# Windowed attention and expert layer on one core: transposing the attention weights with VectorE and SBUF transfers in place of TensorE

## The chip, the core and the metric

The kernel runs on one core of a Trainium2 chip. The engines are named as in the profile: PE (TensorE: matrix products, and transposes as a product with an identity), DVE (VectorE), ACT (ScalarE), POOL (GpSimd) and SP (SyncE, which here issues every transfer). Each engine works through its own queue in order and waits at an instruction whose inputs are not there yet. SBUF is the on-chip memory of 128 partitions, PSUM the memory into which PE writes. The metric is the device time of one execution in microseconds, median of several runs; smaller is better.

## The reference

Four batches, eight heads of 64, 768 positions. Each query sees the keys closer than 16 positions and 24 block summaries (the maximum over 32 keys, the mean over 32 values). The result feeds a gated layer with a squared ReLU.

```python
k_sum = k.reshape(B, H, nb, 32, D).max(axis=3)
v_sum = v.reshape(B, H, nb, 32, D).mean(axis=3)
scores_l = np.where(abs(pos[:, None] - pos[None, :]) < 16, scale * q @ k.T, -1e9)
scores_s = scale * einsum('bhsd,bhnd->bhsn', q, k_sum) + log(32)
a = softmax(concatenate([scores_l, scores_s], axis=-1))
x = (a @ concatenate([v, v_sum], axis=2))      # heads side by side: [4, 768, 512]
xk = mu_k * x + (1 - mu_k) * x_prev
xr = mu_r * x + (1 - mu_r) * x_prev
out = sigmoid(xr @ w_r) * (relu(xk @ w_k) ** 2 @ w_v)
```

## The kernel before

The work falls into **units** and **halves**. A unit (`unit`, L420) is one pair of heads of one batch over one half of the positions, 384 of them: 32 units in all, eight for each batch. It runs like this. `scores` (L441) multiplies queries with 120 columns for each window of 64 queries: 96 neighbouring keys and the 24 block maxima. DVE adds the mask and finds the maximum (L452), ACT takes the exponential (L456), DVE the reciprocal of the sum (L462, L463), POOL scales the weights (L468). The weights `y` now have the queries on the partitions. The product with the values needs the keys there, so PE transposes them: three 128x120 transposes for each head (L475) into the one PSUM buffer `pt`, from where ACT copies them to `pts` (L479). `values` (L488) multiplies `pts` with the values, and DVE or ACT copies the result out (L499, L501).

A half (n = 0 to 7: batch n // 2, first or second half of its positions) is the expert layer: mixing (L510 to L524), the gate (L542 to L544, then the sigmoid L533), and for each of eight chunks a first product (L580), ReLU and square (L587, L589), a split into a high and a low part (L593, L595) and a second product (L606). From half 1 on, a product is made of three in a fast format, out of high and low parts; half 0 uses plain products, which need more time, since the weights have not been split by then (`single`, L567).

Block summaries of the values come, in batch 0, from PE (L380, L400). In batches 1 to 3 they come from a load of the transposed values (L391) into a buffer `st`, a sum on DVE and a small transpose (L395); SP then broadcasts them into the value tiles (L415: 24 rows, six runs of 128 numbers each). The buffers `st`, three of them, are also those into which the weights are loaded (L306).

**What sets the order.** No order is written by hand. `Plan.op` records every operation with its engine, what it reads and writes, and a due time; `Plan.schedule` (L138) then goes through a modelled time and each time issues the operation that can start first, by due time where several can. The lengths come from the table `LENGTH` (L39), the due times from `gate_due`, `e1_due`, `e2_due` and the dues handed to `unit`: half n is due at `GATE1 + PERIOD * (n - 1)`, and the eight units of the next batch are due `UNITS` apart ahead of their gate. Buffers are given out by this plan too. Its result fixes the order on every engine; on the chip the engines wait for each other with semaphores. In the plan, SP needs 60 ns for an issue (L213). `warm` products (L660) fill gaps of PE in the first 110 us of the plan.

Of the kernel before, what the change touches and what calls it, by code (L numbers as in the profile page):

```python
# [20 lines left out]
P = 128  # L21
# [18 lines left out]
    score=900, transpose=340, vtrans=200, vpool=900, vsel=240, spread=560, spread_p=900, values=1000, gate=2790, gate32=930, e1=2090, e1_32=2800,  # L40
    e2a=1400, e2b=700, e2=700, e2_32=2800, e2l_32=930,
    warm=220, kred=860, kred2=470, kmax=190, kcopy=340, vred=860, mask=204, rc=310, evac=475, mixd=535, sub=475, khv=300,
    result=695, wbits=340, wor=612, wsub=612, tiny=60,
    exp=380, pts=380, vm=160, mixa=520, cast=405, relu=525, square=530, sigmoid=500, sigmoid3=4000, wscale=570, wcast=530,
    norm=345, wscale_p=640, wcast_p=640, mixa_p=860, kcopy_p=630, evac_a=375, fill=735,
# [7 lines left out]
STEP0 = 6800  # L53
GATE1 = 92000
PERIOD = 52000
# [4 lines left out]
GAP = 300  # L60
# [40 lines left out]
class Plan:  # L101
# [36 lines left out]
    def schedule(self):  # L138
# [16 lines left out]
        dma = port = 0  # L155
# [10 lines left out]
        while any(ready.values()):  # L166
            best = None
            for e, now in engines.items():
# [3 lines left out]
                for o, at in ready[e]:  # L172
                    if o.name == "warm":
                        fill = max(now, at), o
                        continue
                    start, need, ok = max(at, now, o.due - EARLY if e == "SP" else 0), {}, True
                    for x in o.bufs:
# [14 lines left out]
                    key = (start if late else now, o.due, o.n)  # L192
# [9 lines left out]
            o.cost, o.emit = o.ways[e]  # L202
            for f in o.ways:
                ready[f] = [x for x in ready[f] if x[0] is not o]
# [4 lines left out]
            if e == "PE" and start < COLD:  # L209
                o.cost *= 1.6  # L210
            o.start = start
            if e == "SP":
                engines[e] = start + 60  # L213
                dma = max(dma, start + 600) + o.size * DMA_NS_PER_BYTE
                o.finish = dma + DMA_FIXED - 600
            else:
# [20 lines left out]
def tile_kernel(ctx: ExitStack, tc: tile.TileContext, q, k, vT, v, mask, ident, pool, sel, mu, w_k, w_v, w_r, out):  # L237
# [7 lines left out]
    def slots(name, n, shape):  # L245
# [8 lines left out]
        vs=tiles("vs", 1, [P, NS]), vm=tiles("vm", 4, [P, P]), sp=tiles("sp", 2, [P, P]),  # L254
        y=tiles("y", 4, [P, NSL, NK]), mn=tiles("mn", 4, [P, NSL]), sm=tiles("sm", 3, [P, 2 * NSL]),
        rc=tiles("rc", 3, [P, 2 * NSL]), pts=tiles("pts", 3, [NK, NSL, P]),
# [163 lines left out]
    def unit(b, p, hf, e, due):  # L420
# [9 lines left out]
        pt = [buf("pt") for _ in range(2)]  # L430
        pts = [buf("pts") for _ in range(2)]
# [14 lines left out]
        op("PE", "score", due - 10000, scores, reads=[*e["kparts"], (kt, "s"), (qt, 0)],  # L446
           writes=[(sc[0], 0), (sc[1], 0)])
        for h in range(2):
            for i in range(NSL):
# [3 lines left out]
                    out=y[h].t[:, i, :], in0=sc[h].t[:, i, 0:NK], in1=mask_sb[:, var, :], scale=-SCALE, scalar=3.0e38,  # L453
# [3 lines left out]
                    y[h].t[:, i, :], y[h].t[:, i, :], AF.Exp, bias=mn[h].t[:, i:i + 1], scale=-1.0,  # L457
# [8 lines left out]
        for h in range(2):  # L466
            for i in range(NSL):
                op("POOL", "norm", None, lambda h=h, i=i: nc.gpsimd.tensor_scalar(  # L468
                    out=y[h].t[:, i, :], in0=y[h].t[:, i, :], scalar1=rc.t[:, NSL * h + i:NSL * h + i + 1],
# [3 lines left out]
            def transposes(h=h):  # L473
                for i in range(NSL):
                    nc.tensor.transpose(out=pt[h].t[0:NK, i * P:(i + 1) * P], in_=y[h].t[:, i, :], identity=ident_sb)  # L475
# [3 lines left out]
            op("ACT", "pts", None, lambda h=h: nc.scalar.copy(  # L479
                out=pts[h].t, in_=pt[h].t[0:NK, 0:NSL * P].rearrange("p (i c) -> p i c", c=P)),  # L480
               reads=[(pt[h], 0)], writes=[(pts[h], 0)])

        def values():
            for w in range(HW):
                i, c = divmod(w, 2)
                for h in range(2):
                    hs = slice(h * D, (h + 1) * D)
                    nc.tensor.matmul(  # L488
                        av.t[hs, w * QW:(w + 1) * QW], windows(vw)[:, w, hs], pts[h].t[:, i, c * QW:(c + 1) * QW],
# [14 lines left out]
    def mix(b, hf, which, p):  # L504
# [14 lines left out]
        if first:  # L519
            return xa  # L520
# [44 lines left out]
    def experts(b, hf, x, z):  # L565
# [4 lines left out]
        def first(j):  # L570
# [20 lines left out]
            if single:  # L591
                return
# [189 lines left out]
```

## Time and profile before

| what | value |
|---|---|
| median of 3 runs | 461.58 us (461.45 to 462.07) |
| the profiled execution, whole | 462.56 us |
| its span, first to last instruction | 460.8 us |
| mean granted PE clock | 0.999 |
| PE transposes of weights, L475 | 192, of 128x120 |
| ACT copies of them, L479 | 64, of 120x384 |
| transfers of queue q1 | 24183 packets, 51.35 MB, 32.5% of 16 engines |
| packets under 512 B | 2935 |

The rows of the page and of the trace are shown with the prediction. A row of a group reads: line, engine, operation, output and inputs by the program's names, shapes and count; then busy time and the mean of one in ns; then the idle time of the engine ahead of it and who ended most of it. A row of the chain or of the timeline begins with the start and the length in us. The profiled execution lasts 1.8 us longer than its span.

### The profile page before, as it was taken

Reading aid. Unit: us, or ns where it says so; the run is one execution under the profiler, and the core shown is the slowest. Engines: PE = TensorE matmul, PEld = TensorE weight load, DVE = VectorE, ACT = ScalarE, POOL = GpSimd, SP = SyncE. Lnnn points to the kernel's source line nnn. Section 1 sums busy time; section 2 is a strip of 40 time slices with the busy share of each in tenths; the row PEclk is TensorE's granted clock in tenths of the full one; section 3 lists DMA queues with packets and bytes.
Section 4 is the critical chain, followed back from the end, with each engine's and each line's share of the span. In section 5 each row is a group of like instructions: output and inputs, shape, how many; then the busy total and the mean of one; then the engine's idle time right before and its main releaser. Section 6 shows DMA issues by size and latency. Waiting matters only on the chain.

```text
span 460.8 us, 9597 instructions
## 1 busy us (share of the span) xinstructions
PE 449.6 (98%) x3510; PEld 363.2 (79%) x3510; DVE 254.7 (55%) x846; ACT 288.1 (63%) x811; POOL 112.3 (24%) x238
## 2 busy tenths in 40 slices
PE   8999999988999999999999999999999999999996
PEld 8755655556788888987788888987788889988895
DVE  4789798963642566365444478357364455131213
ACT  3878989876875657258976558248977565232221
POOL 0762565622334002004343002104242201000000
PEclk9999999999999999999999999999999999999999
DMA  8963598652202067036002049017000010001001
GB/s 279 396 228 119 184 324 284 232 209 67 75 8 61 1 224 302 1 91 229 16 14 63 1 130 392 4 43 271 19 16 14 0 70 0 1 1 68 1 0 70
DMA packets 24230, 51.96 MB, mean 113 GB/s; under 512 B 2935, under 2 KB 10743, under 8 KB 24183
## 3 DMA queue, kind: packets, MB, share of 16 engines
q1 hardware_dynamic: 24183, 51.35, 32.5%
q8 instruction: 28, 0.46, 0.4%
q14 instruction: 19, 0.16, 0.1%
HBM read 43.28 MB, written 6.29 MB: 108 GB/s over the span
## 4 chain that ended last, share of the span: by engine, by line
PE 88%; ACT 7%; POOL 2%; SPq 1%; DVE 1%; issue 1%; DMA 0%; POOLq 0%; ACTq 0%
PE mm L606 29%; PE mm L580 28%; PE pt L475 5%; PE av L488 5%; PE sc L441 4%; PE mm L542 4%; PE mm L543 4%; PE mm L544 4%; ACT y L456 3%; PE mm L555 2%; PE pt L660 2%; POOL y L468 2%; ACT L456 1%; ACT pts L479 1%; PE mm L380 1%
## 5 line engine op out<-in xcount | busy, mean ns | idle before, releaser
L580 PE MATMUL mm<-xs,w 128*128 128x384 f32 x736 | 149.8, 352 | 0.0
L580 PEld LDWEIGHTS mm<-xs,w 128*128 128x128 f32 x736 | 130.4, 188 | 12.5 <-issue 1.4
L468 POOL TENSOR_SCALAR y<-y,rc 128x120 f32<-128x120 f32 x192 | 91.2, 493 | 167.5 <-DVE rc L463 138.7
L606 PE MATMUL mm<-w,kh 128*128 128x512 f32 x336 | 91.8, 402 | 0.0
L587 ACT ACTIVATE r<-mm 128x384 f32<-128x384 f32 x64 | 31.2, 487 | 91.9 <-PE mm L580 91.8
L456 ACT ACTIVATE y<-y,mn 128x120 f32<-128x120 f32 x192 | 73.5, 385 | 12.2 <-DVE mn L452 11.9
L606 PEld LDWEIGHTS mm<-w,kh 128*128 128x128 f32 x336 | 60.7, 188 | 11.2 <-issue 0.2
L593 DVE CAST kh<-r 128x384 fp32r<-128x384 f32 x44 | 16.1, 365 | 75.2 <-ACT r L589 75.1
L452 DVE CUSTOM_DVE_ANT_0 y<-sc,mask_sb 128x120 f32<-128x120 f32 x192 | 42.4, 277 | 25.1 <-PE sc L441 22.7
L606 PE MATMUL mm<-w,kl 128*128 128x512 f32 x168 | 52.3, 406 | 0.0
L524 DVE TENSOR_TENSOR xs<-xa,xs 128x384 fp32r<-128x384 f32 x56 | 30.1, 552 | 29.5 <-ACT xs L522 29.2
L479 ACT COPY pts<-pt 120x384 f32<-120x384 f32 x64 | 30.3, 474 | 14.8 <-PE pt L475 13.3
L516 DVE SCALAR_TENSOR_TENSOR xa<-vx,mu_sb,xa 128x384 f32<-128x384 f32 x56 | 33.7, 628 | 6.2 <-ACT xa L510 5.4
L456 ACT ACTIVATION_READ_ACCUMULATOR y<-y,mn 128x1 f32 x192 | 36.2, 189 | 0.0
L475 PE MATMUL pt<-ident_sb,y 128*120 128x128 f32 x192 | 32.7, 279 | 3.0 <-POOL y L468 2.5
L542 PE MATMUL mm<-w,xs 128*128 128x512 f32 x84 | 33.6, 399 | 2.0 <-ACT z L533 2.0
L606 PEld LDWEIGHTS mm<-w,kl 128*128 128x128 f32 x168 | 30.1, 188 | 6.1
L589 ACT ACTIVATE r<-r 128x384 f32<-128x384 f32 x64 | 33.6, 524 | 1.1
L488 PEld LDWEIGHTS av<-pts,vx 120*64 120x64 f32 x768 | 25.2, 137 | 11.4 <-issue 10.0
L475 PEld LDWEIGHTS pt<-ident_sb,y 128*120 128x120 f32 x192 | 22.3, 137 | 15.1 <-POOL y L468 6.4
L595 DVE TENSOR_TENSOR kl<-r,kh 128x384 fp32r<-128x384 f32 x56 | 31.8, 568 | 4.1 <-ACT kh L594 1.1
L544 PE MATMUL mm<-w,xs 128*128 128x512 f32 x84 | 32.8, 391 | 0.0
(66 smaller groups left out, 539.7 us busy)
## 6 DMA issues: line engine op xcount, KB each, us to landing
vx<-in_v SPq DMA_DIRECT2D x32, 384.0 KB
kt<-in_k SPq DMA_DIRECT2D x15, 544.0 KB
qt<-in_q SPq DMA_DIRECT2D x32, 192.0 KB
out<-z SPq DMA_DIRECT2D x24, 256.0 KB
st<-in_vT SPq DMA_DIRECT2D x12, 384.0 KB
st<-in_w_k SPq DMA_DIRECT2D x8, 512.0 KB
st<-in_w_v SPq DMA_DIRECT2D x8, 512.0 KB
st<-in_w_r SPq DMA_DIRECT2D x4, 512.0 KB
```

Source lines behind the costliest of these rows:

```text
L452: op("DVE", "mask", None, lambda h=h, i=i, var=var: nc.vector.tensor_tensor_reduce(out=y[h].t[:, i, :], in0=sc[h].t[:, i, 0:NK], in1=mask_ ...
L456: op("ACT", "exp", None, lambda h=h, i=i: nc.scalar.activation(y[h].t[:, i, :], y[h].t[:, i, :], AF.Exp, bias=mn[h].t[:, i:i + 1], scale=-1.0,
L468: op("POOL", "norm", None, lambda h=h, i=i: nc.gpsimd.tensor_scalar(out=y[h].t[:, i, :], in0=y[h].t[:, i, :], scalar1=rc.t[:, NSL * h + i: ...
L475: nc.tensor.transpose(out=pt[h].t[0:NK, i * P:(i + 1) * P], in_=y[h].t[:, i, :], identity=ident_sb)
L479: op("ACT", "pts", None, lambda h=h: nc.scalar.copy(out=pts[h].t, in_=pt[h].t[0:NK, 0:NSL * P].rearrange("p (i c) -> p i c", c=P)), reads= ...
L488: nc.tensor.matmul(av.t[hs, w * QW:(w + 1) * QW], windows(vw)[:, w, hs], pts[h].t[:, i, c * QW:(c + 1) * QW], start=True, stop=True,)
L516: op("DVE", "mixd", None, lambda: nc.vector.scalar_tensor_tensor(out=xa.t, in0=xt.t[:, 1 + lo:1 + lo + HT], scalar=mu_sb[:, which, p:p + 1 ...
L542: nc.tensor.matmul(ps.t, xh.t[:, ts], h, start=(p == 0), stop=False)
L544: nc.tensor.matmul(ps.t, xl.t[:, ts], h, start=False, stop=(p == NPAIR - 1))
L580: nc.tensor.matmul(ps.t[:, 0:HT], w.t[:, p * P:(p + 1) * P], (x[p] if single else x[p][s]).t, start=(n == 0), stop=(n == len(terms) * NPAI ...
L589: op("ACT", "square", None, lambda: nc.scalar.activation(r.t, r.t, AF.Square), reads=[(r, 0)], writes=[(r, 0)])
L606: nc.tensor.matmul(acc[t].t, a.t[:, t * P:(t + 1) * P], v.bitcast(F32) if single else v, start=start, stop=stop)
```

## The change

In batches 1 to 3 the weights are no longer transposed by PE. The tile `y` gets 128 columns in place of 120 (eight zeros each, set once by POOL). DVE transposes each head's 128x384 weights within blocks of 32x32 into a buffer `st`, two instructions a unit (`flip`). That leaves each block transposed where it stood; block (r, c) has yet to go to row block r, column block c. Sixteen transfers a unit, all issued by SP, do that (`move`): one for each pair (c, r), 32 partitions (24 for the last r) by six runs of 32 numbers. The values then read `pts`, of which there are two whole ones (one unit each). Batch 0 keeps PE's transposes and ACT's copies. In the first half, six of the eight chunks stay plain, and two use the split form (`PLAIN`), so that its mixed inputs are split too. The table of lengths, the due times and the scheduler's rules change: an issue on SP costs 450 ns in the plan, at most eight transfers are under way, and a change of ACT's function table has a price.

```diff
+    norm=345, wcast_p=640, mixa_p=600, kcopy_p=450, evac_a=375, flip=470,
...
-STEP0 = 6800
-GATE1 = 92000
-PERIOD = 52000
+STEP0 = 4800
+PLAIN = 6, 6
+GATE1 = 80000
+PERIOD = 51000
...
-EARLY = 15000
+EARLY = 20000
+AHEAD = 22000
+ISSUE = 450
+LANES = 8
+TABLE = 1300
+TABLES = dict(sigmoid=1, sigmoid3=1, exp=0, wscale=0)
...
-SECOND = 9000
-UNITS = 6000
+SECOND = 40000, 50000, 60000, 70000
+UNITS = 6500
...
+                    if o.name == "wcast" and len(free_slots["w"]) < owed + 2:
+                        continue
...
+                    if e == "SP":
+                        start = max(start, lanes[-LANES])
...
-                    key = (start if late else now, o.due, o.n)
+                    load = e == "ACT" and TABLES.get(o.name, table) != table
+                    key = (start if late else now, o.due + TABLE * load, o.n)
...
-                engines[e] = start + 60
+                engines[e] = start + ISSUE
...
-        y=tiles("y", 4, [P, NSL, NK]), mn=tiles("mn", 4, [P, NSL]), sm=tiles("sm", 3, [P, 2 * NSL]),
-        rc=tiles("rc", 3, [P, 2 * NSL]), pts=tiles("pts", 3, [NK, NSL, P]),
+        y=tiles("y", 4, [P, NSL, P]), mn=tiles("mn", 4, [P, NSL]), sm=tiles("sm", 3, [P, 2 * NSL]),
+        rc=tiles("rc", 3, [P, 2 * NSL]), pts=tiles("pts", 2, [P, 2, NSL, P]),
...
-        op("PE", "score", due - 10000, scores, reads=[*e["kparts"], (kt, "s"), (qt, 0)],
+        op("PE", "score", due - (10000 if b == 0 else AHEAD), scores, reads=[*e["kparts"], (kt, "s"), (qt, 0)],
...
+            if b > 0:
+                continue
             op("PE", "transpose", due - 3500 + 800 * h, transposes,
...
+        if b > 0:
+            yt = buf("st", U32, False)
...
+            for h in range(2):
+                op("DVE", "flip", due - AHEAD + 8000 + 500 * h, lambda h=h: nc.vector.transpose(
+                    out=flipped()[:, h * NSL:(h + 1) * NSL, :], in_=y[h].t),
+                   reads=[(y[h], i) for i in range(NSL)], writes=[(yt, h)])
+            blocks = [(c, r) for c in range(4) for r in range(4)]
+            for n, (c, r) in enumerate(blocks):
+                rows = min(32, NK - 32 * r)
+                op("SP", "move", due - 4500 - ISSUE * (len(blocks) - 1 - n), lambda c=c, r=r, rows=rows: nc.sync.dma_start(
+                    out=spots()[32 * r:32 * r + rows, :, 32 * c:32 * c + 32],
+                    in_=flipped()[32 * c:32 * c + rows, :, 32 * r:32 * r + 32]),
+                   reads=[(yt, 0), (yt, 1)], writes=[(pts, f"m{n}")], size=32 * 2 * NSL * 128)
...
-        single = b + hf == 0
+        plain = PLAIN if b + hf == 0 else (0, 0)
...
+            single = j < plain[0]
+            kh, kl = ks[j] = (r, None) if j < plain[1] else (buf("kh", F32R), buf("kl", F32R))
...
+    for t in pools["y"]:
+        op("POOL", "tiny", None, lambda t=t: nc.gpsimd.memset(t[:, :, NK:P], 0.0))
```

What this does to the order is seen on three queues. First PE in batch 2, before: one unit's last transposes among the second and first products of an expert chunk (`pt` the PSUM buffer, `y` the weights, `kh` and `kl` the high and low parts of an activation).

```order
L606 MATMUL mm1_133<-w34_0_805,kh1_119 128x512
L606 MATMUL mm1_133<-w38_0_855,kh1_119 128x512
L606 MATMUL mm0_132<-w34_0_805,kh1_119 128x512
L606 MATMUL mm0_132<-w38_0_855,kh1_119 128x512
L475 MATMUL pt0_130<-ident_sb_137,y1_92 120x128 x3
L606 MATMUL mm3_135<-w34_0_805,kl1_121 128x512
L606 MATMUL mm1_133<-w34_0_805,kl1_121 128x512
L606 MATMUL mm0_132<-w34_0_805,kl1_121 128x512
```

And PE in batch 2 now: a unit's values (`av`, read from one `pts`), then the second products of a chunk.

```order
L528 MATMUL av0_129<-pts1_105,vx5_73 64x64 x12
L651 MATMUL mm1_131<-w35_0_900,kh1_117 128x512
L651 MATMUL mm1_131<-w15_1_1020,kh1_117 128x512
L651 MATMUL mm3_133<-w35_0_900,kh1_117 128x512
L651 MATMUL mm3_133<-w15_1_1020,kh1_117 128x512
L651 MATMUL mm0_130<-w35_0_900,kh1_117 128x512
L651 MATMUL mm0_130<-w15_1_1020,kh1_117 128x512
L413 MATMUL pt0_128<-ident_sb_135,vs0_84 24x128
L651 MATMUL mm1_131<-w35_0_900,kl1_119 128x512
```

No transposes of weights stand between the products any more; only the small transpose of the block sums still writes `pt`. Second, SP around the units of batch 2, before: loads of queries, keys and values, two broadcasts, stores.

```order
L346 DMA vx5_73<-in_v 128x768
L415 DMA vx0_68<-vm0_85 24x6x128
L415 DMA vx3_71<-vm0_85 24x6x128
L346 DMA vx8_76<-in_v 128x768
L424 DMA qt1_65<-in_q 128x384
L342 DMA kt1_62<-in_k 128x1088
L640 DMA out_0<-z0_108 128x512
```

SP in batch 2 now, at the end of one unit's moves (`pts0` from `st0`) and the start of the next one's (`pts1` from `st1`).

```order
L518 DMA pts0_104<-st0_120 32x6x32 x3
L518 DMA pts1_105<-st1_121 32x6x32
L518 DMA pts0_104<-st0_120 24x6x32
L518 DMA pts1_105<-st1_121 32x6x32 x2
L518 DMA pts1_105<-st1_121 24x6x32
L518 DMA pts1_105<-st1_121 32x6x32 x3
L518 DMA pts1_105<-st1_121 24x6x32
L685 DMA out_0<-z0_106 128x512
L433 DMA vx1_69<-vm0_85 24x6x128
L518 DMA pts1_105<-st1_121 32x6x32
L685 DMA out_0<-z1_107 128x512
```

The moves of two units overlap in the queue, and broadcasts and stores stand among them; 384 moves come to the 166 transfers that SP had. Third, DVE in batch 2 now: the reciprocals of one unit, then block transposes of a unit's two heads, a copy of a unit's result, mixing, and the masks of the next unit.

```order
L480 TENSOR_SCALAR sm0_98<-sm0_98 128x6
L481 RECIPROCAL rc0_101<-sm0_98 128x6
L539 COPY vx10_78<-av0_129 128x384
L512 STREAM_TRANSPOSE st2_122<-y0_90 128x384
L567 TENSOR_TENSOR xs1_1_893<-xa0_110,xs0_1_888 128x384
L556 SCALAR_TENSOR_TENSOR xa1_111<-vx10_78,mu_sb_136,xa1_111 128x384
L512 STREAM_TRANSPOSE st2_122<-y1_91 128x384
L470 ISA y2_92,mn0_94<-sc0_126,mask_sb_134 128x120
```

The block transposes are new in DVE's queue, behind the reciprocal that POOL's scaling needs and ahead of masks and copies that PE's next steps need.

More of the change, by code (lines that the diff above doesn't have):

```diff
@@ L39 @@
 LENGTH = dict(
[L40 to L45, printed above, removed]
+    score=865, transpose=350, vtrans=200, vpool=800, vsel=330, spread=540, spread_p=900, values=930, gate=2740, gate32=930, e1=2100,
+    e1_32=2690, e2a=1400, e2b=705, e2=705, e2_32=2600, e2l_32=930,
+    warm=223, kred=865, kred2=470, kmax=90, kcopy=280, vred=865, mask=204, rc=320, evac=470, mixd=535, sub=475, khv=280,
+    result=600, wbits=340, wor=610, wsub=605, tiny=60,
+    exp=380, pts=375, vm=160, mixa=515, cast=405, relu=380, square=425, sigmoid=500, sigmoid3=1600, wscale=570, wcast=530,
+    norm=345, wcast_p=640, mixa_p=600, kcopy_p=450, evac_a=375, flip=470,
 )
@@ L154, in schedule @@
         ready = {e: [] for e in engines}
-        dma = port = 0
+        dma = port = table = 0
+        lanes = [0] * LANES
+        owed = sum(o.name == "wor" for o in self.ops)
         order = []
@@ L210, in schedule @@
                 o.cost *= 1.6
+            if e == "ACT" and TABLES.get(o.name, table) != table:
+                o.cost += TABLE
+                table = 1 - table
             o.start = start
             if e == "SP":
-                engines[e] = start + 60
+                engines[e] = start + ISSUE
                 dma = max(dma, start + 600) + o.size * DMA_NS_PER_BYTE
                 o.finish = dma + DMA_FIXED - 600
+                lanes.append(o.finish)
             else:
@@ L429, in unit @@
         sm, rc = buf("sm"), buf("rc")
-        pt = [buf("pt") for _ in range(2)]
-        pts = [buf("pts") for _ in range(2)]
+        pts = buf("pts")
+        pt = [buf("pt") for _ in range(2)] if b == 0 else None
         av = buf("av")
@@ L474, in transposes @@
                 for i in range(NSL):
-                    nc.tensor.transpose(out=pt[h].t[0:NK, i * P:(i + 1) * P], in_=y[h].t[:, i, :], identity=ident_sb)
+                    nc.tensor.transpose(out=pt[h].t[0:NK, i * P:(i + 1) * P], in_=y[h].t[:, i, 0:NK], identity=ident_sb)
+            if b > 0:
+                continue
             op("PE", "transpose", due - 3500 + 800 * h, transposes,
@@ L488, in values @@
                     nc.tensor.matmul(
-                        av.t[hs, w * QW:(w + 1) * QW], windows(vw)[:, w, hs], pts[h].t[:, i, c * QW:(c + 1) * QW],
+                        av.t[hs, w * QW:(w + 1) * QW], windows(vw)[:, w, hs], pts.t[0:NK, h, i, c * QW:(c + 1) * QW],
                         start=True, stop=True,
                     )
-        op("PE", "values", due - 1000, values, reads=[(vw, x) for x in "ab"] + [(pts[0], 0), (pts[1], 0)],
+        op("PE", "values", due - 1000, values, reads=[(vw, x) for x in "ab"] + [(pts, x) for x in ([f"m{n}" for n in range(16)] if b else range(2))],
            writes=[(av, 0)])
@@ L519, in mix, with halves @@
         if first:
-            return xa
+            return (xa,)
+        return halves(xa)
+    def halves(xa):
         xh, xl = buf("xs", F32R), buf("xs", F32R)
@@ L600, in second @@
             kh, kl = ks[j]
+            single = kl is None
             due = e2_due(b, hf, j)
@@ L668, in tile_kernel @@
     x = mixes(0, 0, 0)
+    if PLAIN[0] < NCV:
+        x = [(xa, *halves(xa)) for xa, in x]
     for p in range(NPAIR):
-        unit(0, p, 1, sets[p], gate_due(0, 1) - 9000 - (NPAIR - 1 - p) * SECOND)
-    experts(0, 0, x, z)
+        unit(0, p, 1, sets[p], SECOND[p])
     for i in range(NCK):
@@ L676, in tile_kernel @@
         split("wv", j)
+    experts(0, 0, x, z)
     for n in range(1, 2 * B):
```

36 lines of the change are left out of this document (20 added, 16 removed).

## The prediction

> **What bounds the kernel now.** I read the page first: the busy times, then the chain that ended last.
>
> ```profile
> span 460.8 us, 9597 instructions
> PE 449.6 (98%) x3510; PEld 363.2 (79%) x3510; DVE 254.7 (55%) x846; ACT 288.1 (63%) x811; POOL 112.3 (24%) x238
> PE 88%; ACT 7%; POOL 2%; SPq 1%; DVE 1%; issue 1%; DMA 0%; POOLq 0%; ACTq 0%
> ```
>
> TensorE stands still for 460.8 - 449.6 = 11.2 us only. A microsecond taken from its queue shortens the run, provided that nothing else becomes late. Where are those 11.2 us, and who else is short of time? The busy times by stage (columns: stretch, its length, PE, PEld, DVE, ACT, POOL, clock, DMA share, GB/s):
>
> ```profile
> 42.00:98.00 56.00, 56.00 (x404) 32.97 (x402) 49.12 (x152) 49.45 (x144) 31.71 (x49) 1.00 0.76 257
> 98.00:113.00 15.00, 11.33 (x112) 8.16 (x111) 6.91 (x32) 11.89 (x32) 4.53 (x13) 1.00 0.19 71
> 206.00:260.00 54.00, 53.35 (x539) 44.54 (x533) 29.10 (x122) 42.62 (x131) 18.93 (x45) 1.00 0.23 74
> ```
>
> From 206 to 260, where the attention units of batch 2 run between the experts, PE is full (53.35 of 54.00). At 98 to 113 it lacks 3.7 us. The granted clock is 1.00, so it explains nothing here.
>
> **What the change removes.** One step of PE is, in the chain, the time by which it puts off the next:
>
> ```profile
> 88.72 0.11 PE pt L395
> 115.01 0.33 PE pt L475 x3
> 115.34 0.78 PE sc L441 x24
> 117.17 0.85 PE av L488 x24
> 56.67 2.58 PE mm L606 x6
> 60.82 2.58 PE mm L580 x8
> 189.92 2.11 PE mm L580 x12
> 192.03 2.10 PE mm L606 x9
> 208.14 0.23 PE mm L542
> ```
>
> Three transposes of a head cost 0.33 us. Batches 1 to 3 have 24 units of two heads: 48 x 0.33 = **15.8 us** less on PE. In the first half of batch 0 two of eight expert chunks go from the plain form (2.58 us for each product) to the split one (2.11 and 2.10): 2 x (0.47 + 0.48) = **1.9 us** less. The groups priced below (busy, mean ns) say what else goes and comes.
>
> ```profile
> L479 ACT COPY pts<-pt 120x384 f32<-120x384 f32 x64 | 30.3, 474 | 14.8 <-PE pt L475 13.3 <-PE pt L660 1.4
> L499 DVE COPY vx<-av 128x384 f32<-128x384 f32 x11 | 6.1, 555 | 7.2 <-PE av L488 7.2
> L593 DVE CAST kh<-r 128x384 fp32r<-128x384 f32 x44 | 16.1, 365 | 75.2 <-ACT r L589 75.1
> ```
>
> ACT loses 48 copies of 474 ns, 22.8 us; it waits elsewhere for PE, so I count nothing. DVE gains 48 block transposes of 128x384. The trace has none; DVE copies of that size take 365 to 555 ns, and I take 0.55: 16 a batch are 8.8 us, inside the 24.9 us that DVE has free between 206 and 260. In front of a transpose stands a wait for POOL's scaling of y; masks, casts and subtractions queue behind it on DVE, and PE waits for those, but the order puts it some rows behind rc, where POOL has begun. The split chunks add conversions between 42 and 98, where ACT and DVE are seven eighths busy: I add **1 us**. Filling matmuls (60 now, 51 before) run only in gaps.
>
> **What it adds: the SP queue.** A unit's 16 moves must be issued one after the other before its values can run, and loads, stores and broadcasts stand in the same queue. This is the unknown. The rows of SP (ns minimum, median, maximum; below them start and length in us):
>
> ```profile
> L415 SPq DMA_DIRECT2D vx<-vm x24: 778/788/951, 89.6 to 353.5; - x24
> L306 SPq DMA_DIRECT2D st<-in_w_k x8: 327/328/331, 25.3 to 74.2; - x8
> L346 SPq DMA_DIRECT2D vx<-in_v x32: 327/432/1026, 4.0 to 315.3; - x32
> 112.27 1.66 SPq L415 DMA_DIRECT2D vx<-vm  x2
> 114.02 0.47 SPq L640 DMA_DIRECT2D out<-z  x1
> ```
>
> A load of 128 rows takes 0.33 us where SP was idle, 0.43 behind other big loads. The broadcast of 24 rows takes 0.79. Two of those need 1.66, so 0.04 a piece lies between issues. Twelve moves of a unit have 32 rows, four have 24, all with six runs of 32 numbers a row. Why is L415 dear? Its completions differ (packets in a stretch with two broadcasts, and in one with the last stores):
>
> ```profile
> DMA packets 312, 0.15 MB, mean 49 GB/s; under 512 B 24, under 2 KB 312, under 8 KB 312
> q1 hardware_dynamic: 312, 0.15, 26.7%
> DMA packets 432, 0.79 MB, mean 207 GB/s; under 512 B 48, under 2 KB 48, under 8 KB 432
> ```
>
> Two broadcasts of 24 x 6 runs leave 288 packets and 24 tiny ones, 12 each; three stores of 128 rows leave 384 and 48, 16 each. So 24 rows go over 12 engines, 32 can go over 16 like the loads. The bounds for any move are 0.33 and 0.79 x 192/144 = 1.05 us (by L415's runs). Between them I take for 24 rows L415's own 0.79 + 0.04 = 0.83, and for 32 rows the loads' 0.33 + 0.04 = 0.37, since what stands before is small: 12 x 0.37 + 4 x 0.83 = **7.8 us** a unit, 0.48 a move. No row of this trace separates the twelve engines from the third dimension or from the source that is read six times.
>
> Does SP keep up? I compare both queues over seven units of batch 2 in the changed order, from the second unit's scores to the eighth's values. PE holds 7 scores, 7 values, 12 first products, 105/9 second ones, 36 gate matmuls and 4 small transposes (0.11): 5.5 + 6.0 + 25.3 + 24.5 + 8.3 + 0.4 = 70.0 us. What PE really takes is longer than such a sum; first and last values of batch 2 before, and one unit's scores and scaling:
>
> ```profile
> 206.33 0.92 PE L488 MATMUL av<-pts,vx 120*64 120x64 f32 x24
> 259.51 0.92 PE L488 MATMUL av<-pts,vx 120*64 120x64 f32 x24
> 236.17 0.85 PE L441 MATMUL sc<-kt,qt 64*64 64x120 f32 x24
> 240.87 2.88 POOL L468 TENSOR_SCALAR y<-y,rc 128x120 f32<-128x120 f32 x6 [4.90 <-DVE rc L463]
> ```
>
> 53.2 us, against 50.4 by the sum of the same prices over what the order before holds there: 1.055. So 73.8 us. Scores to the end of scaling are 7.6 us, the last block transpose 0.55: the moves can begin 8.2 us after the scores, which leaves 65.6 us. SP must issue 84 moves of 32 rows (31.1), 28 of 24 (23.2), 8 broadcasts (6.6) and 7 loads and stores (7 x 0.43 = 3.0): 63.9. From the end of an issue to landing (no packets, then half busy):
>
> ```profile
> 112.20:113.60 1.40, 1.21 (x8) 1.25 (x9) 0.00 (x0) 0.52 (x2) 0.17 (x1) 1.00 0.00 0
> 113.60:114.40 0.80, 0.80 (x7) 0.80 (x6) 0.00 (x0) 0.00 (x0) 0.00 (x0) 1.00 0.50 92
> ```
>
> The first broadcast, issued 112.27 to 113.06, has landed by about 114.4: 1.3 us. Together 65.2 against 65.6 us: **SP just keeps up**. That is a balance on a knife's edge: each 0.1 us more for a move of 32 rows is 8.4 us a batch, some 25 us in the run. Each transfer also waits for the one eight before it, but eight issues take 3.8 us and one lives 2.1 us.
>
> The packets: 26.7% of 16 engines over 3 us for 312 packets is 41 ns each at 512 B. A unit's 12 x 192 + 4 x 144 = 2880 runs of 128 B cost 2880/16 x 41 = 7.4 us at most, a quarter of it if bytes count; I take 4, beside 9 us of issuing. Its cover is that issuing; without it the dear price would stand beside the 7.6 us that PE needs for a unit (53.2 us for seven).
>
> **Sum.** 15.8 + 1.9 - 1.0 = 16.7 us less. The profiled execution took 462.56 us (1.8 outside its span), the median is 461.58; from that 461.6 - 16.7 = **445 us**.
>
> **Rivals.**
> (1) *An issue behind an issue.* The store right behind a broadcast took 0.47 us, not 0.33. At 0.51 with its gap SP needs 42.8 + 23.2 + 6.6 + 3.0 + 1.3 = 76.9 us, 11.3 too many a batch: 461.6 - 16.7 + 34 = **479**. For it: moves stand in rows of sixteen. Against: loads of 128 rows with 327 ns.
> (2) *The third dimension is what costs.* Then all moves have L415's price: 112 x 0.83 + 6.6 + 3.0 + 1.3 = 103.9 us, 38.3 too many; PE waits for its values in all three batches: 461.6 - 16.7 + 115 = **560**, slower. It decides from a mean price of 0.54 us a move on, where the three batches lose 16.7. For it: L415 is the only other transfer with rows of six runs. Against: its 12 engines and its repeated source are reasons as good. At 1.05 us it would be about 625.
> (3) *Runs set the issue.* A move has 192 runs, a load 128: 0.33 x 1.5 + 0.04 = 0.53, SP 78.6 us, 13.0 too many a batch: **484**. L415 needs 0.79 for 144, so runs alone don't explain it. The Trainium skill (same page and section) says that the slice lasts while descriptors are generated, which is this rival; that neither 0.33 nor 0.79 follows their number speaks against it.
> (4) *A run costs two accesses.* The Trainium skill (DMA: Bandwidth & Descriptors, Specifications) wants 512 B for the line rate and says that the engines read, modify and write below it. As a mechanism here: each run of 128 B twice the 41 ns, 14.8 us a unit; seven units are 104 us on the engines, as long as SP in (2): again about **560**. No row of this trace shows a run of that size by itself, so it keeps a small chance.
> (5) *Nothing to be had:* SP a little late eats the gain, **461**, at some 0.44 us for 32 rows.
>
> **How the numbers follow.** Forecast 445: 0.55, own range 438 to 457 (the unseen start up to 113 us, where the order changes most, and a few hundredths an issue). (1) 0.17, (2) 0.12, (3) 0.07, (4) 0.03, (5) 0.06. Low 438 is the sum with the 3.7 us at 98 to 113 gone and 3 more; high 490 takes in (1), (3) and (5), and leaves (2) and (4) out. A measurement tells 0.2%, 0.9 us, from no change. Faster: the forecast, 0.55; within: 0.06, from (5); slower: 0.39.
>
> **What would show it.** Right: moves of 32 rows near 0.33 us on SP, the chain still PE for 88% or more, transposes of batch 0 alone left (16 groups), DVE transposes near 0.55. Wrong: values that wait for DMA, SP issuing without a pause, PE busy falling below 95% while batches 1 to 3 run. The length of a move on SP decides between the forecast, (1), (2) and (3); moves that are short there and values that wait all the same would be (4).

## The result, and the profile after

The kernel after the change takes **566.94 us** (563.79 to 569.31), beside 461.82 us before: a ratio of 1.226 [1.218, 1.234]. The forecast was 445 with a range of 438 to 490. The profiled execution took 563.79 us, 1.8 of them outside its span. Times and ratios here are of runs at the usual speed; one run of the last experiment, 466.25 us, was in a slower state and is left out.

The page after: the span, PE's busy time, the clock in 40 slices, the packets of the transfer queue, the chain by engine and by line, and the groups of the values (L528) and of the block transposes (L512).

```profile
span 562.0 us, 9938 instructions
PE 473.3 (84%) x3398; PEld 385.2 (69%) x3398; DVE 277.1 (49%) x897; ACT 271.6 (48%) x770; POOL 106.5 (19%) x242
...
PEclk9999999898887889979788889997878789999999
...
q1 hardware_dynamic: 99063, 60.22, 36.9%
...
PE 44%; SPq 26%; DMA 12%; DVE 6%; issue 6%; ACT 3%; POOL 2%; DVEq 0%; POOLq 0%
SPq L518 24%; PE mm L651 13%; PE mm L624 11%; PE av L528 5%; DMA kt<-in_k 4%; DMA pts<-st 4%; PE mm L585 3%; PE mm L586 3%; PE mm L587 3%; DMA vx<-vm 2%; PE sc L459 2%; ACT y L474 2%; POOL y L486 2%; PE mm L598 2%; SPq L433 1%
...
L528 PE MATMUL av<-pts,vx 120*64 120x64 f32 x768 | 39.8, 256 | 80.4 <-issue 34.0
...
L512 DVE STREAM_TRANSPOSE st<-y 128x384 f32<-128x384 f32 x48 | 26.4, 564 | 42.6 <-DMA pts<-st 40.5
```

The costliest line of the chain is no longer a product but L518, the moves' issue on SP, with 24%; PE's share falls from 88 to 44%. PE stands still for 562.0 - 473.3 = 88.7 us, 77.5 more than before, and 80.4 of it stands in front of the values. The "issue" in that row is time for which the profile shows no wait of PE's own; the weight loads of the same line (PEld) appear below among those that waited for the moves.

The moves on SP (ns minimum, median, maximum), and who waited for them (us, times):

```profile
L518 SPq DMA_DIRECT2D pts<-st x384: 585/604/1657, 83.1 to 466.2; - x192
...
who waited for it (us, times):
  PE av L528: 52.3, 12
  DVE st L512: 40.5, 10
  PEld av L528: 21.9, 5
```

A move takes 0.604 us at the median and never less than 0.585. The next three fences are pieces of the timeline of batch 2 (start and length in us). First SP's queue: the first unit's moves, the start and the end of the rest.

```profile
218.05 11.30 SPq L518 DMA_DIRECT2D pts<-st  x16
229.46 0.45 SPq L442 DMA_DIRECT2D qt<-in_q  x1
...
231.94 8.39 SPq L518 DMA_DIRECT2D pts<-st  x9
240.44 0.83 SPq L433 DMA_DIRECT2D vx<-vm  x1
241.32 5.57 SPq L518 DMA_DIRECT2D pts<-st  x7
...
322.15 3.71 SPq L518 DMA_DIRECT2D pts<-st  x5
325.90 0.52 SPq L360 DMA_DIRECT2D kt<-in_k  x1
326.47 0.43 SPq L442 DMA_DIRECT2D qt<-in_q  x1
326.94 0.83 SPq L433 DMA_DIRECT2D vx<-vm  x1
```

Sixteen moves take 11.30 us, 0.71 each with the gap behind them; 0.48 was expected. Two of them, one of 32 and one of 24 rows, in the chain of waits:

```profile
222.25 0.60 SPq L518
222.90 0.83 SPq L518
```

The next one starts 0.65 us after the first, so 0.05 lies between. Then PE: the scores of the second unit, two units' values in the middle of the stage, and the last values of the batch. Last, DVE: the block transposes of the second unit.

```profile
220.56 0.84 PE L459 MATMUL sc<-kt,qt 64*64 64x120 f32 x24
...
269.35 1.68 PE L528 MATMUL av<-pts,vx 120*64 120x64 f32 x24 [7.10 <-DMA pts<-st]
...
277.02 1.17 PE L528 MATMUL av<-pts,vx 120*64 120x64 f32 x24 [1.27 <-DVE mn L470]
...
331.23 1.15 PE L528 MATMUL av<-pts,vx 120*64 120x64 f32 x24 [2.86 <-DMA vx<-vm]
```

```profile
230.87 1.04 DVE L512 STREAM_TRANSPOSE st<-y 128x384 f32<-128x384 f32 x2 [4.84 <-DMA pts<-st]
```

These rows split the stretch for which the prediction compared PE and SP, from the second unit's scores to the start of the eighth's values: 331.23 - 220.56 = 110.7 us.

| piece | predicted | measured |
|---|---|---|
| scores to the first move | 8.2 | 231.94 - 220.56 = 11.4 |
| SP's queue, 112 moves and what stands between | 63.9 | 325.86 - 231.94 = 93.9 |
| last issue to the last values | 1.3 | 331.23 - 325.86 = 5.4 |
| together | 73.4 | 110.7 |

Thirty of the 37 us too many are the queue itself. Three are a wait that I did not have at all: the second unit's block transposes wait 4.84 us for a `st` buffer, until the moves of an earlier unit have read it. Four come from the last broadcast, issued behind the moves and two loads. Three batches at 37.3 are 112 us; with the forecast's 445 that gives 557. Ten of the measured 567 are left; batches 1 and 3 were not taken apart in this way.

The windows of two unit stages and of the end (columns as in the prediction; the clock is the third number from the end):

```profile
218.00:313.00 95.00, 72.95 (x571) 61.19 (x570) 38.38 (x152) 42.54 (x134) 17.26 (x47) 0.87 0.31 70
...
360.00:470.00 110.00, 85.92 (x629) 71.98 (x628) 44.27 (x164) 47.66 (x146) 16.66 (x45) 0.84 0.32 72
470.00:562.00 92.00, 88.03 (x444) 77.31 (x444) 30.57 (x60) 28.40 (x57) 1.91 (x2) 1.00 0.07 26
```

Where units run, PE is busy for three quarters of the time, at a clock of 0.84 to 0.87, with the transfer engines at a third. Where only experts are left, it is full again at 1.00. PE's busy time rose by 23.7 us although 17.7 us of work left it, so some 41 us are slower products, by estimate most of them the clock's. The clock at two units' values, behind the waits of 7.10 and of 1.27 us:

```profile
269.35:271.03 1.68, 1.68 (x25) 1.55 (x25) 0.00 (x0) 0.00 (x0) 0.00 (x0) 0.50 0.61 184
277.02:278.19 1.17, 1.14 (x26) 0.96 (x26) 0.00 (x0) 1.09 (x3) 0.00 (x0) 1.00 0.20 32
```

The first had half the clock. The second had the full one, so that its 1.17 us, beside 0.92 before the change, are not the clock's doing; what they are is open. In batches 1 to 3 all values behind a wait of 4.2 us or more had a mean clock of 0.50 to 0.53, all behind 3.7 us or less 0.89 to 1.00. The Trainium skill (TensorE: Matmul & The Clock Gate, HAM oscillation — how this bites in real kernels) warns of PE idle gaps above about 3.4 us, after which the clock falls; these figures agree roughly. Whether that clock costs the run anything was a question for an experiment.

### The profile page after: what moved, and what is told of

Read it like the earlier page. It is cut to its first block, busy times and chain, and to the rows that moved or that the text cites. A ratio compares the mean times of both kernels' runs of the same rounds, so it can differ in the third digit from the quotient of the medians.

```text
span 562.0 us, 9938 instructions
## 1 busy us (share of the span) xinstructions
PE 473.3 (84%) x3398; PEld 385.2 (69%) x3398; DVE 277.1 (49%) x897; ACT 271.6 (48%) x770; POOL 106.5 (19%) x242
## 3 DMA queue, kind: packets, MB, share of 16 engines
q1 hardware_dynamic: 99063, 60.22, 36.9%
## 4 chain that ended last, share of the span: by engine, by line
PE 44%; SPq 26%; DMA 12%; DVE 6%; issue 6%; ACT 3%; POOL 2%; DVEq 0%; POOLq 0%
SPq L518 24%; PE mm L651 13%; PE mm L624 11%; PE av L528 5%; DMA kt<-in_k 4%; DMA pts<-st 4%; PE mm L585 3%; PE mm L586 3%; PE mm L587 3%; DMA vx<-vm 2%; PE sc L459 2%; ACT y L474 2%; POOL y L486 2%; PE mm L598 2%; SPq L433 1%
## 5 line engine op out<-in xcount | busy, mean ns | idle before, releaser
L624 PE MATMUL mm<-xs,w 128*128 128x384 f32 x744 | 158.8, 365 | 0.0
L624 PEld LDWEIGHTS mm<-xs,w 128*128 128x128 f32 x744 | 141.8, 202 | 10.7 <-issue 0.9
L528 PE MATMUL av<-pts,vx 120*64 120x64 f32 x768 | 39.8, 256 | 80.4 <-issue 34.0
L651 PE MATMUL mm<-w,kh 128*128 128x512 f32 x348 | 106.4, 438 | 0.2 <-ACT kh L638 0.2
L528 PEld LDWEIGHTS av<-pts,vx 120*64 120x64 f32 x768 | 33.9, 163 | 94.4 <-issue 63.6
L474 ACT ACTIVATE y<-y,mn 128x120 f32<-128x120 f32 x192 | 73.4, 384 | 47.7 <-DVE mn L470 47.6
L651 PEld LDWEIGHTS mm<-w,kh 128*128 128x128 f32 x348 | 70.6, 210 | 15.8 <-issue 0.9
L512 DVE STREAM_TRANSPOSE st<-y 128x384 f32<-128x384 f32 x48 | 26.4, 564 | 42.6 <-DMA pts<-st 40.5
L553 POOL TENSOR_SCALAR xa<-vx,om_sb 128x384 f32<-128x384 f32 x14 | 11.1, 795 | 169.1 <-DVE xs L567 168.0
L541 ACT COPY vx<-av 128x384 f32<-128x384 f32 x23 | 11.0, 480 | 60.3 <-PE av L528 60.2
L567 DVE TENSOR_TENSOR xs<-xa,xs 128x384 fp32r<-128x384 f32 x56 | 30.3, 551 | 15.4 <-ACT xs L565 15.4
L550 ACT ACTIVATE xa<-vx,om_sb 128x384 f32<-128x384 f32 x42 | 25.0, 612 | 19.2 <-DVE xs L567 12.9
```

Source lines behind the costliest of these rows:

```text
L474: op("ACT", "exp", None, lambda h=h, i=i: nc.scalar.activation(y[h].t[:, i, 0:NK], y[h].t[:, i, 0:NK], AF.Exp, bias=mn[h].t[:, i:i + 1], s ...
L528: nc.tensor.matmul(av.t[hs, w * QW:(w + 1) * QW], windows(vw)[:, w, hs], pts.t[0:NK, h, i, c * QW:(c + 1) * QW], start=True, stop=True,)
L567: op("DVE", "sub", None, lambda: nc.vector.tensor_tensor(out=xl.t, in0=xa.t, in1=xh.t.bitcast(F32), op=ALU.subtract), reads=[(xa, 0), (xh, ...
L624: nc.tensor.matmul(ps.t[:, 0:HT], w.t[:, p * P:(p + 1) * P], x[p][s].t, start=(n == 0), stop=(n == len(terms) * NPAIR - 1))
L651: nc.tensor.matmul(acc[t].t, a.t[:, t * P:(t + 1) * P], v.bitcast(F32) if single else v, start=start, stop=stop)
```

## The experiments

The theory from this profile: the issue of a move on SP costs 0.65 us with its gap and not 0.37, SP is the bound while units run, and all other waits follow from that. Rivals: the new order and plan are at fault; the third dimension, the number of runs or the 24-row moves make the price; the falling clock makes the time.

**The plan without the moves.** PE's transposes and ACT's copies in all batches, all else as after the change; scores of batches 1 to 3 are due 14 us before the unit instead of 22.

```diff
-        pt = [buf("pt") for _ in range(2)] if b == 0 else None
+        pt = [buf("pt") for _ in range(2)]
...
-            if b > 0:
-                continue
...
-        if b > 0:
+        if False:
             yt = buf("st", U32, False)
...
```

> The changed kernel with its new scheduler, but with the transposes of batches 1 to 3 on TensorE again and no moves (scores of these batches due 14 us ahead of the unit, not 22). Theory A (the issue of the moves on SP is the bound): no moves, so 452 to 466 us, granted clock 0.99 or more, PE idle near 11 us. Rival C (the new table of lengths and due times is what costs): well above 480 us although no move is left.

456.76 us, 0.990 [0.988, 0.991] of the kernel before, clock 1.00, PE's busy time:

```profile
PE 447.5 (98%) x3520; PEld 365.2 (80%) x3520; DVE 257.8 (57%) x853; ACT 293.4 (64%) x823; POOL 105.7 (23%) x237
```

The new order, table of lengths and split chunks are not at fault; alone they gain 4.9 us. The due time of 22 us ahead for the scores, which this run leaves out, stands in the next one.

**The moves taken out.** The values of batches 1 to 3 read the block-transposed tile as it stands: the blocks are not put in place, and the 16 transfers of a unit are left out. Block transposes, due times and buffers of `st` stay; the `pts` of these batches go.

```diff
-                        av.t[hs, w * QW:(w + 1) * QW], windows(vw)[:, w, hs], pts.t[0:NK, h, i, c * QW:(c + 1) * QW],
+                        av.t[hs, w * QW:(w + 1) * QW], windows(vw)[:, w, hs], (flipped()[0:NK, h * NSL + i] if b else pts.t[0:NK, h, i])[:, c * QW:(c + 1) * QW],
...
```

> The changed kernel without its moves: block transposes as before, and the values read their output as it stands (the blocks are not put in place: that part of the computation is left out). If the moves on SP are all that the change costs, this is what it would give with moves for nothing: the prediction's 445 us (438 to 450), clock 0.99 or more, DVE and ACT hidden. If block transposes, the new order or the buffers cost by themselves: above 455 us.

441.35 us, 0.957 [0.955, 0.958]. The page:

```profile
span 440.3 us, 9344 instructions
PE 431.7 (98%) x3382; PEld 351.2 (80%) x3382; DVE 274.6 (62%) x891; ACT 275.4 (63%) x779; POOL 105.7 (24%) x241
...
PEclk9999999999999999999999999999999999999999
...
L512 DVE STREAM_TRANSPOSE st<-y 128x384 f32<-128x384 f32 x48 | 26.0, 562 | 7.6 <-POOL y L486 6.6
```

PE is full again at full clock. So everything above 441 comes with the moves: 566.9 - 441.4 = 125.6 us. The block transposes keep their length and lose the wait for `st` (40.5 us after, none here). Between this kernel and the one with PE's transposes lie 456.8 - 441.4 = 15.4 us, and 447.5 - 431.7 = 15.8 us of PE's busy time: the saving on PE by itself.

**All moves of 32 rows.**

```diff
-                rows = min(32, NK - 32 * r)
+                rows = 32
```

> The moves of 24 rows are made 32 rows long (the eight rows more are zeros that nothing reads). Theory A: these 4 of 16 issues fall from about 0.83 to 0.60 us, 0.9 us a unit, some 6 us a batch on SP, with the clock's share 535 to 553 us. Rival B (the transfers themselves, their runs on the DMA engines, are the bound): 7% more runs, so the time stays or rises, 563 to 580 us.

550.04 us, 1.192 [1.189, 1.195]. The 24-row moves explain 17 of the 105 us that the kernel lost, and no more. All 384 moves, added up from the two traces, now hold SP for 244.2 us in place of 259.8, so the gain is about the issue time saved.

**A third of the runs.** Each move carries two of its six runs a row; four of a unit's six weight tiles are left out.

```diff
-                    out=spots()[32 * r:32 * r + rows, :, 32 * c:32 * c + 32],
+                    out=spots()[32 * r:32 * r + rows, 0:2, 32 * c:32 * c + 32],
...
```

> Each move carries only the first two of its six runs (the weights of four of six blocks a unit are left out): as many issues, a third of the runs, still three dimensions. Theory A with the third dimension as its price: slices of a move stay 0.58 to 0.60 us and the run stays near 567 us (550 to 575). Theory A with the number of runs as its price: slices fall to about 0.4 us and the run to 470 to 500 us. Rival B: slices stay, but the run falls to 480 to 520 us, since a third of the packets is left.

One run, 560.16 us. The page's packets, and the moves:

```profile
q1 hardware_dynamic: 52983, 54.32, 30.9%
```

```profile
L518 SPq DMA_DIRECT2D pts<-st x384: 585/598/1682, 83.8 to 462.6; - x192
```

With 64 runs in place of 192 a move still takes 0.598 us, and with 46080 packets fewer the kernel still takes 560. Neither the number of runs nor the packets set the price. By the Trainium skill (Perfetto Trace Analysis, DMA Instruction — HWDGE), which rival (3) of the prediction draws on, the slice holds the generation of the descriptors. For transfers that POOL issues, the Trainium skill (DMA: Bandwidth & Descriptors, Anatomy of one DMA — SWDGE (gpsimd) path) says that many descriptors can be emitted before that shows. The row shows the same for SP's transfers, from 64 to 192 runs.

**No third dimension.** The layouts of `st` and `pts` are rearranged so that the six runs of a row lie together, and a move is one run of 768 B a row.

```diff
-                    out=spots()[32 * r:32 * r + rows, :, 32 * c:32 * c + 32],
-                    in_=flipped()[32 * c:32 * c + rows, :, 32 * r:32 * r + 32]),
+                    out=spots()[32 * r:32 * r + rows, c].rearrange("p n c -> p (n c)"),
+                    in_=flipped()[32 * c:32 * c + rows, r].rearrange("p n c -> p (n c)")),
...
```

> The block transposes write and the values read a layout in which the six runs of a row lie one behind the other, so that a move is two-dimensional: 32 (or 24) rows of one run of 768 B; as many issues and bytes. Theory A with the third dimension or the runs as its price: 32 rows 0.33 to 0.37 us, 24 rows about 0.57, a unit 7 us of SP, SP keeps up, clock 0.99, 443 to 460 us. If the price were a move's own, whatever its shape: slices stay 0.60 and the time near 567 us. The layout may cost DVE or PE something: block transposes above 0.56 us or values above 0.85 us would show it.

549.22 us, 1.193 [1.188, 1.199].

```profile
L519 SPq DMA_DIRECT2D pts<-st x384: 507/588/1956, 83.3 to 451.7; - x192
```

This missed: I had expected the loads' price once the shape was a load's. The minimum falls by 0.08 us, the median by 0.02, and all moves together from 259.8 to 244.9 us of SP, about the 17.7 us that the kernel gains. Runs of 768 B are also above the 512 B of the rival on small runs, and the time does not come back. Shape is not the main cause; the endpoints were left.

**The price measured by itself.** The kernel before, with 28 small transfers of 768 B a row behind its last store, four of each of these kinds. Their results are not used.

```diff
+    KINDS = [
+        lambda w: (scr[:, w], k[0, 0, :, 0:192]),
+        lambda w: (scr[0:32, w], k[0, 0, 0:32, 0:192]),
+        lambda w: (scr[0:24, w], k[0, 0, 0:24, 0:192]),
+        lambda w: (scr[:, w], src[:, 0:192]),
+        lambda w: (scr[0:32, w], src[0:32, 0:192]),
+        lambda w: (scr[32:64, w], src[0:32, 0:192]),
+        lambda w: (scr[0:24, w], src[0:24, 0:192]),
+    ]
...
```

> The kernel before, with 28 small transfers behind its last store, each made to wait for the one before it: four each of 128, 32 and 24 rows of 768 B from HBM, then 128, 32, 32 (into partitions 32 to 63) and 24 rows of 768 B from SBUF to SBUF. Their results are not used. What makes a move dear? If a source in SBUF does: 128 rows from SBUF near 0.5 to 0.6 us, 32 rows from HBM 0.33. If few rows do: 32 rows from HBM near 0.55, 128 rows from SBUF 0.33. If only the queue behind the last issue does: all 32 and 128 rows 0.33, since each stands alone. 24 rows 0.2 us above 32 rows in every case (12 engines).

One run. The transfers out of HBM (`in_k`) and out of SBUF (`y`), both into SBUF, and the same kernel's stores out of SBUF into HBM:

```profile
L703 SPq DMA_DIRECT2D scr<-y x16: 465/578/807, 467.5 to 480.3; - x16
L703 SPq DMA_DIRECT2D scr<-in_k x12: 297/322/453, 456.7 to 466.4; - x12
```

```profile
L640 SPq DMA_DIRECT2D out<-z x24: 332/343/473, 112.5 to 456.3; - x24
```

The 28 in order, in ns:

```
HBM to SBUF, 128 rows               453 452 328 378
HBM to SBUF, 32 rows                335 319 311 325
HBM to SBUF, 24 rows                303 298 297 297
SBUF to SBUF, 128 rows              567 595 465 465
SBUF to SBUF, 32 rows               609 565 508 507
SBUF to SBUF, 32 rows to 32 to 63   590 591 507 507
SBUF to SBUF, 24 rows               807 744 714 714
```

This is the cause, as far as one run with one order of the kinds can show it. A transfer of the same 32 rows and bytes takes 0.32 us when it comes out of HBM and 0.51 when both ends are in SBUF; 24 rows go from 0.30 to 0.71. A store, SBUF to HBM, has 0.34 with 128 rows, so a source in SBUF alone is not dear: it is both ends. A store of 32 rows was not measured. In the kernel the flat moves come down to the same 0.507 and the moves with six runs a row to 0.585, so the third dimension adds at most 0.08; at the median it adds 0.02.

The expectation has each transfer wait for the one before. The trace shows otherwise: they run mostly in pairs, the second issued 0.04 to 0.26 us behind the first, before the first has moved its packets. The HBM kinds run alike, so the difference is not this. And the third of each kind out of SBUF is issued after SP has been idle for 0.4 to 0.8 us, at 465, 508, 507 and 714 ns: an issue right behind an issue is not needed for the price.

**The plan told the true price.** All moves of 32 rows, and 645 ns for an issue in the plan.

```diff
-ISSUE = 450
+ISSUE = 645
```

> Moves of 32 rows throughout, and the scheduler reckons with 645 ns an issue, as measured (0.604 and its gap), in place of 450. Theory A (SP's issues are the bound, and PE stands in its queue behind values planned too early): a batch needs 128 x 0.645 + 8 x 0.86 + some 20 x 0.45 = 98 us of SP of a period near 100, so the moves can nearly hide once the order is right: 480 to 520 us, granted clock 0.95 or more. If capacity and not the order sets the time: 540 to 550, as with rows of 32 alone.

546.23 us, 1.184 [1.181, 1.186]: 4 us better than with 450, where I had expected 30 to 70. Knowing the price, this scheduler made no room in the queue. That does not settle it for every order. After the change SP is full only while a batch's units run; between the units of two batches it issues next to nothing, as here, ahead of the first moves of batch 3:

```profile
340.49 0.43 SPq L364 DMA_DIRECT2D vx<-in_v  x1
350.14 0.33 SPq L442 DMA_DIRECT2D qt<-in_q  x1
350.51 0.43 SPq L364 DMA_DIRECT2D vx<-in_v  x1
358.19 4.14 SPq L518 DMA_DIRECT2D pts<-st  x6
```

By the expectation a batch needs 98 us of SP, while PE's 431.7 us without moves are 108 a batch. An order that spreads the moves over the whole batch might hide them; it was not tried.

**A quarter of the moves less.** As the last, and the four blocks on the diagonal, which stay in their own partitions, are copied by POOL; 12 moves a unit.

```diff
+                if c == r:
+                    op("POOL", "diag", None, lambda c=c: nc.gpsimd.tensor_copy(
+                        out=spots()[32 * c:32 * c + 32, :, 32 * c:32 * c + 32],
+                        in_=flipped()[32 * c:32 * c + 32, :, 32 * c:32 * c + 32]),
+                       reads=[(yt, 0), (yt, 1)], writes=[(pts, f"m{n}")])
+                    continue
```

> As e5_plan645, and the four blocks of a unit that stay where they are (r = c) are copied by POOL: 12 moves a unit. Theory A: 96 x 0.645 + 8 x 0.86 + 9 = 78 us of SP a batch, so that little of it shows: 450 to 475 us, clock 0.98 or more. Rival (the order, not SP's capacity, costs): about the same as e5_plan645.

469.37 us, 1.017 [1.016, 1.019]. The page:

```profile
PE 443.2 (95%) x3390; PEld 358.7 (77%) x3390; DVE 278.4 (59%) x899; ACT 271.8 (58%) x771; POOL 143.1 (31%) x337
...
PE 63%; ACT 10%; DMA 8%; SPq 8%; DVE 6%; issue 3%; POOL 2%; POOLq 0%; ACTq 0%; DVEq 0%
```

A quarter of the issues away, and of the 85 us by which the last kernel stood above the one before the change 77 are gone. Seven units now need 84 x 0.65 = 54.6 us for moves in place of 72.8; with the 10.9 us of broadcasts, loads and landing that is 65.5, just what the prediction had free for SP. So the steep loss ends about where the prediction's weighing of SP's queue against PE's, with the right price in it, puts the edge. But by that sum no loss would be left, and the kernel is still 28 us above the one without moves. Nor do the 96 issues of 0.65 us, 62 us in all, make up the 77; what the rest is was not tried.

**Filling PE's waits.** After the change, with 12 products of zeros put ahead of each unit's values in batches 1 to 3, to keep the clock up.

```diff
+            for _ in range(12 if b else 0):
+                nc.tensor.matmul(pools["pt"][0][:, 512 - P:512], zero_sb, zero_sb, start=True, stop=True)
```

> The changed kernel with 12 filling products (128x128, about 2.9 us at full clock) on PE ahead of the values of each unit of batches 1 to 3, which write an unused part of a PSUM buffer. PE is busy 24 us longer in what were waits. If the falling PE clock costs time of its own: clock from 0.91 to 0.95 or more and 545 to 560 us. If it is a mere sign of the waiting and SP sets the pace: 563 to 575 us.

566.9 us, 1.229 [1.227, 1.231], with a mean clock of 0.973 beside 0.911. PE's busy time and the filling products:

```profile
PE 516.5 (92%) x3974; PEld 434.1 (77%) x3974; DVE 277.4 (49%) x897; ACT 271.4 (48%) x770; POOL 106.4 (19%) x242
L525 PE MATMUL pt<-zero_sb 128*128 128x128 f32 x576 | 68.5, 275 | 0.0
```

Without the filling PE is busy for 516.5 - 68.5 = 448.0 us, 16 above the 431.7 without moves; after the change it was 42 above. Most of the clock came back and the time did not: while SP sets the pace, a faster product only waits longer. The slower clock is a symptom here.

**Both remedies together, and a second queue.** The flat layout, all moves of 32 rows, POOL's diagonal blocks and 600 ns in the plan:

```diff
-ISSUE = 450
+ISSUE = 600
...
+                if c == r:
+                    op("POOL", "diag", None, lambda c=c: nc.gpsimd.tensor_copy(
+                        out=spots()[32 * c:32 * c + 32, c].rearrange("p n c -> p (n c)"),
+                        in_=flipped()[32 * c:32 * c + 32, c].rearrange("p n c -> p (n c)")),
...
```

> As e8_diag with the flat layout of e4_flat (one run of 768 B a row) and 600 ns an issue in the scheduler: 12 moves a unit of about 0.51 to 0.59 us. Theory A (issues on SP): some 0.05 us less for each of 96 moves a batch, 5 us a batch, 450 to 466 us against e8_diag's 469. If landing of small runs were what is left in e8_diag (DMA 8% of its chain), a larger fall, below 450 us.

474.43 us, 1.030 [1.025, 1.035]: a miss, and 5 us worse than POOL's diagonal alone. It changed the layout and the plan's number at once, so which of them lost that is open. Then the same with three of the 12 moves issued by ACT:

```diff
+                if c == 3:
+                    op("ACT", "move_a", None, lambda c=c, r=r, rows=rows: nc.scalar.dma_start(
...
```

> As e9_flatdiag, with three of the twelve moves issued from ACT's queue. If the price belongs to SP's own queue, SP has a quarter less to do, 443 to 460 us, and ACT's issues take 0.5 to 0.6 us each (14 us a batch, in which exponentials and copies wait). If the price belongs to a generator that both queues share, the SP slices grow where both issue, and the time is that of e9_flatdiag or worse.

492.71 us, 1.066 [1.061, 1.071], a miss as well. The moves on SP and on ACT:

```profile
L531 SPq DMA_DIRECT2D pts<-st x216: 507/589/1889, 84.5 to 384.5; - x108
```

```profile
L526 ACTq DMA_DIRECT2D pts<-st x72: 514/520/1054, 85.7 to 381.1; - x72
```

An issue costs on ACT 0.520 us at the median, somewhat less than on SP, and SP's median does not rise beside it. But the exponentials, ReLUs and mixing of ACT now stand behind its moves, in the one queue that it works through in order: added up over the trace, ACT was idle for 22.7 us until a move had landed, in the kernel with all moves on SP for 2.1. That this is where the 18 us went was not tried by itself.

**Every second unit.** PE's transposes stay for the units of the first half of the positions in all batches; the others are moved, all in 32 rows, with 645 ns in the plan.

```diff
+        moved = b > 0 and hf == 1
...
```

> In batches 1 to 3 only every second unit (the second half's) has its weights turned by DVE and moved, in 16 transfers of 32 rows; the other units keep PE's transposes and ACT's copies. The plan counts 645 ns for an issue. Theory (SP's queue is what could not keep up, and nothing else is wrong with the moves): SP now has 64 moves a batch of 0.65 us, 42 us, with 11 us of broadcasts, loads and landing, 53 us in the 65 that there are. So it keeps up, and 24 of the 48 pairs of transposes are saved on PE against the kernel with PE's transposes everywhere (456.8): 24 x 0.33 = 7.9 us, 449 (446 to 453), faster than before by 2 to 3%, clock 0.99 or more, SPq under 3% of the chain. Rival (a unit that waits for its own moves costs PE whatever the queue's load, by in-order waits and buffers): the gain is eaten, 457 or more, with SPq or DMA holding over 5% of the chain and the clock under 0.99.

458.94 us (456.51 to 461.86), 0.992 [0.989, 0.994]: a miss of the theory by 10 us, and, but for the clock, what the rival said. The page of the run of 461.86 us, and its values' waits for transfers (us, times, longest):

```profile
PE 442.0 (96%) x3446; PEld 360.1 (78%) x3446; DVE 270.6 (59%) x880; ACT 283.1 (62%) x790; POOL 116.1 (25%) x247
...
PE 68%; SPq 11%; DMA 8%; ACT 7%; DVE 3%; issue 2%; ACTq 0%
```

```profile
PE av L529 <- DMA pts<-st: 5.0, 4, 2.5
PE av L529 <- DMA vx<-vm: 3.1, 2, 2.4
```

PE has 5.5 us less to do than with its transposes everywhere (447.5), and idles for 18.1 us in place of 8.2. The clock stays at 0.996, so waits long enough to halve it are rare; but SP still holds 11% of the chain, and 8.1 us of waits for single units' moves and broadcasts eat the saving. That the queue's sum fits into the stage is not enough: a unit's own 10 us of moves can still be late for its values.

The fastest kernel here that computes the whole reference is the plan without the moves, 456.76 us: faster than the one before and the one after. No kernel with moves has a median below 458.94; 441 is the limit at which they would cost nothing.

## Why the prediction was wrong, point by point

- **What bounds the kernel, and what leaves PE: right.** 15.8 us of transposes were predicted, 15.4 lie between the kernel without moves and that with PE's transposes. The rest of the plan gained 4.9 us where I had 0.9 (1.9 for the split chunks less 1.0 for conversions); which of its parts did was not tried.
- **The block transposes: right.** 0.564 us each for 0.55, and they cost nothing with the moves gone.
- **"What stands before is small", 0.33 + 0.04 = 0.37 us for a move of 32 rows: the step that failed.** It measured 0.604 with 0.045 behind it, 0.65 us. The 24-row price was 0.83 with its gap, and 0.83 and 0.05 were measured. Of the bounds 0.33 and 1.05 I took the end of the loads, which come out of HBM. The only row of that trace with both ends in SBUF was L415, and the prediction lists three reasons why it is dear: twelve engines, the third dimension, the source read six times. The one that counted, both ends in SBUF, is not among them, though `vx<-vm` says so. In the runs the third dimension is worth at most 0.08 us, and 24 rows are dear with both ends in SBUF only.
- **SP against PE: a useful sum with the wrong price in it, and not the whole.** It named 0.54 us a move as the point from which the saving is lost; the moves took 0.71. With the measured price the sum is 112 x 0.71 = 79.5, with 10.9 us of the rest 90.4 in place of 65.2: 25 us too many a batch, 74 in all, 519. Measured are 48 more. The split of batch 2 shows where 12 of them come from, and the other batches likely have theirs: more loads and pauses in the queue, block transposes that wait for `st`, and a last broadcast behind the moves. Where the sum just fits, 28 us of loss were left (12 moves a unit), so the overlap that it takes as complete is not.
- **The moves' packets: right that they hide.** The transfer engines were at 36.9%, and with two thirds of the moves' packets gone the time was 560.
- **The rivals.** An issue behind an issue (479) and the number of runs (484) had too low a price and the wrong mechanism. A run that costs two accesses (560) has the right time by luck, and falls with the shorter and the longer runs. The third dimension (560) had nearly the right time and the right consequence, PE waiting for its values in all three batches, by a mechanism that falls with the flat layout. Its chance of 0.12 was too small mainly because I gave prices above 0.54 so little weight between bounds of 0.33 and 1.05.
- **What would show it.** Every sign named for "wrong" came: moves at 0.60, SP without a pause while a batch's units run, values that wait for DMA, PE at 77% from 218 to 313 us.

## What to carry to other kernels

Take the price of an issue from a row with the same two memories at its ends; where none exists, keep the dear end of the bounds alive. Then sum the issuing queue over the stage in which its results are needed, with the buffers that its source holds meanwhile: when that sum passes the engine it feeds, fewer issues help (a quarter fewer gave 77 us here), and telling the scheduler the price or moving fewer runs hardly did. Work moved off a full engine has to be cheap on a queue with real slack, since even half of the moves cost in waits what they saved.

## What was new about the hardware

- The issue of a small transfer on SP, with little else under way: 0.30 to 0.33 us from HBM to SBUF for 24 and 32 rows, 0.47 to 0.51 from SBUF to SBUF for 128 and 32 rows, 0.71 for 24 rows (the last two of four each; 567 to 807 ns for the first two out of SBUF). Why both ends in SBUF cost this was not found.
- Fewer rows can be dearer: 24 rows need 0.2 us more than 32 with both ends in SBUF, and no more than 32 out of HBM.
- PE's clock fell to 0.84 to 0.87 in stages with waits of 4 to 7 us, and a unit's values behind such a wait took 1.67 us at half the clock, beside 0.92 before. Products of zeros kept the mean of the run at 0.973 without any gain.
